# Where the remaining fill units and the first token block's preparation stand, how the first pair begins, and where the rms weight is multiplied

## The chip, the cores and the metric

The kernel runs on one core of a Trainium2 chip. Its engines each work through their own instructions in a fixed order: PE (TensorE) multiplies matrices, PEld is PE's weight load, DVE (VectorE), ACT (ScalarE) and POOL (GpSimd) work on tiles, and SP (SyncE) and ACT issue DMAs, in line with whatever else stands on that engine. An instruction starts when the one before it on its engine lets it and what it waits for on other engines or DMAs is done. The metric is the time of one execution in microseconds (us); lower is better.

## The reference

Linear attention over 8 batches, 8 heads, 576 tokens of 64 dimensions, with 128 random features; its output, as 4608 tokens of 512 channels, goes through an rms norm and a gated layer with 1536 hidden channels. w_gate, w_val, w_out and rms_g follow below as `w_*` and `rms_g`; q, k, v and w_phi are 32-bit floats, the gated layer's weights come as 64-bit floats.

```python
def phi(x):
    proj = np.einsum('bhsd,df->bhsf', x, w_phi)
    proj = proj - np.max(np.abs(proj), axis=-1, keepdims=True)
    return np.concatenate([np.exp(proj), np.exp(-proj)], axis=-1)
q_p, k_p = (phi(q), phi(k))
kv = np.einsum('bhsf,bhsd->bhfd', k_p, v)
z = np.sum(k_p, axis=2)
num = np.einsum('bhsf,bhfd->bhsd', q_p, kv)
den = np.einsum('bhsf,bhf->bhs', q_p, z)[..., None] + 1e-06
x = (num / den)                       # as (B*S, H*D)
rms = np.sqrt(np.mean(x * x, axis=-1, keepdims=True) + 1e-06)
xn = x / rms * rms_g
g = xn @ w_gate
silu = g * (1.0 / (1.0 + np.exp(-g)))
val = xn @ w_val
return (silu * val @ w_out).astype(np.float32)
```

## The kernel before, in words

All products that matter are made from a high and a low part: an operand is cast (`_split`, line 60, on ACT mostly) and the low part is what the cast left over (line 61, DVE or POOL), and a product takes three matmuls.

**Attention** goes over 32 pairs of heads (four per batch) in a pipeline of four steps. In turn i of the main loop `front(i)` transposes k, q and the rests (`rb`, the last 64 tokens of k and q) on PE (L298), projects them (L311 to L313) and takes the largest size off (L315, L318, DVE; tiles `yk`, `yq`, `yr`); `mid(i-1)` makes the exponentials (ACT L338, L342, L375, L376; the low parts `ql` on POOL L380) and sums k's features times v into `acc` (L346, L351), which it splits into `kv0` and `kv1` (h and l); `back(i-2)` makes the numerators and denominators (PE L415, ACT L417) and sends the denominators out and back through memory so that they lie on 64 partitions (`dd`, `dr`, `di`, `rc`: SP L419, L423, L426, L428, with the reciprocal L425 on DVE between); `last(i-3)` divides (`fin`, DVE L442, L443) and stores the result to `xs` (SP). `_merge` puts the pieces of the four steps into one order by their places in the turn.

**Decoding.** The 64-bit weights are turned into 32-bit ones by whole-tile operations (`_decode`, L48 to L55: ACT, DVE, POOL), one piece per turn. The first eight pieces are the first 384 columns of w_gate and w_val; each is then multiplied by the rms weight `g` on DVE (L235) and split into `wf1`.

**Fill.** The products of these 384 columns don't need the rms of x, so they run during attention: `fill` splits a block of 288 tokens of `xs` (16 blocks; `xo`), and each of its six units is 12 matmuls (L474) into a PSUM tile `fp` (two buffers, which `num` and `prep` use too), a copy on ACT (L477, `fo`, three buffers) and a DMA to `gvs` (L478, on SP). `load_x` loads the next blocks on ACT's queue (L142), into one of two x buffers by the block's parity. `quota` hands out units so that some 30 are left when attention ends; the `while` loop does those.

**Preparation.** `prep(bk, x, ...)` (L145 to L165) makes the rms of a block of 384 tokens: four squares on ACT (L147, L150) added on POOL (L151), a sum over the channels on PE (L156, L157), the root on ACT (L159, with a table load), the reciprocal and the scaling on DVE (L160, L162), a cast on ACT and the low part on POOL (tile `xb`). The first block's, `prep(0)`, stands in turn 29 (`PR - 3`), its load in turn 27; `load_x` pauses in between.

**After attention** come the gated layer's other nine column groups for 12 blocks (`gv`, PE L588, with weights loaded through `wc`, ACT queue L564) and the output product (L742). None of that code changes.

A scheduler puts the program's pieces into each engine's order as it expects them to be ready; `late()` ties what stands in it behind the last instructions written so far on ACT, DVE and POOL.

## Time and profile before

| | us |
|---|---|
| time, median of 3 executions | 1333.65 (1332.86 to 1335.17) |
| the profiled execution | 1339.35 |
| its span, first to last instruction | 1337.6 |
| PE busy in it | 1288.5 (96%) |
| PE's mean granted clock | 0.992 |

The profile is of one execution of its own. Rows of the timeline give start, duration, engine, line, operation, tile written and tiles read, and in brackets how long the engine was idle ahead of it and what ended that. Rows of stretches give start and end, length, then the busy time of PE, PEld, DVE, ACT and POOL with counts, PE's granted clock as a share of full speed, the share of the DMA engines and GB/s. A wait row gives who waited for whom, the total, the times and the longest. Line numbers are those of the kernel before.

### The profile page before, as it was taken

What the parts mean: (1) busy time and instruction counts of PE and PEld (TensorE: products, weight loads), DVE (VectorE), ACT (ScalarE), POOL (GpSimd) and SP (SyncE); (2) the same over time, 40 slices, a digit from 0 to 9 for tenths busy, and PEclk for the clock granted to TensorE, in tenths of its full rate; (3) what the DMA queues carried; (4) which work ended last, traced back from release to release, by engine and by line L of the source; (5) the groups of instructions that cost most, each with busy time, mean ns of one, the idle gap of its engine ahead of it and who ended that gap; (6) DMA issues with size and microseconds to landing.
All of it is one profiled execution on the core that took longest, in us unless ns stands there. A gap on an engine that the chain in (4) does not pass through costs nothing.

```text
span 1337.6 us, 25479 instructions
## 1 busy us (share of the span) xinstructions
PE 1288.5 (96%) x9396; PEld 1275.6 (95%) x9396; DVE 885.0 (66%) x1301; ACT 711.0 (53%) x1510; POOL 605.5 (45%) x568
## 2 busy tenths in 40 slices
PE   7989999999999896899999999999999999999998
PEld 7989899999999896899999999999999999999998
DVE  7899788778778773313456656655534498777784
ACT  5988877778778782434344344443333334434332
POOL 3766565555555570000233223233221078788684
PEclk9999999999999898999999999999999999999999
DMA  5555556566555434843454454554433534554451
GB/s 159 127 147 156 161 158 165 167 170 169 157 164 161 123 95 127 249 153 126 141 170 140 157 168 133 166 168 140 133 115 108 183 111 126 150 166 127 142 168 54
DMA packets 204524, 197.22 MB, mean 147 GB/s; under 512 B 69552, under 2 KB 186416, under 8 KB 204400
## 3 DMA queue, kind: packets, MB, share of 16 engines
q1 hardware_dynamic: 186448, 181.44, 45.2%
q10 hardware_dynamic: 17952, 14.16, 3.8%
q8 instruction: 74, 1.21, 0.4%
q14 instruction: 50, 0.41, 0.1%
HBM read 126.04 MB, written 69.50 MB: 146 GB/s over the span
## 4 chain that ended last, share of the span: by engine, by line
PE 57%; DMA 3%; DVE 1%; ACT 0%; issue 0%; POOL 0%; ACTq 0%; SPq 0%; DVEq 0%
PE fp L588 17%; PE gp L588 16%; PE gd L742 6%; PE gz L742 6%; PE gy L742 5%; PE fp L474 4%; PE fp L742 3%; DMA wc<-wvs 1%; DMA gvs<-fo 1%; DMA rc<-di 0%; PE sm L415 0%; DMA dd<-nd 0%; ACT fo L477 0%; POOL s2l L61 0%; DVE a12l L61 0%
## 5 line engine op out<-in xcount | busy, mean ns | idle before, releaser
L380 POOL TENSOR_TENSOR ql<-eq,qh 128x256 fp32r<-128x256 f32 x256 | 217.7, 882 | 67.3 <-issue 39.5
L588 PE MATMUL gp<-xb,wv 128*128 128x384 f32 x864 | 161.9, 334 | 0.8 <-ACT wv L60 0.8
L588 PE MATMUL fp<-xb,wg 128*128 128x384 f32 x864 | 161.0, 334 | 0.0
L573 DVE TENSOR_TENSOR h<-sl,gp 128x384 f32<-128x384 f32 x108 | 59.6, 552 | 144.2 <-PE gp L588 75.6
L588 PEld LDWEIGHTS gp<-xb,wv 128*128 128x128 f32 x864 | 150.7, 188 | 1.0 <-ACT wv L60 1.0
L571 ACT ACTIVATE sl<-fp 128x384 f32<-128x384 f32 x108 | 52.8, 489 | 185.6 <-PE fp L588 170.7
L588 PEld LDWEIGHTS fp<-xb,wg 128*128 128x128 f32 x864 | 150.7, 188 | 0.0
L54 POOL TENSOR_TENSOR wa<-raw,wa 128x192 f32<-128x192 f32 (+1 forms) x112 | 66.2, 613 | 162.2 <-issue 58.6
L351 PE MATMUL acc<-vm,ek 128*128 128x65 f32 x1024 | 131.8, 271 | 0.0
L315 DVE TENSOR_REDUCE mx<-pp 128x4 f32<-128x512 f32 (+1 forms) x160 | 100.6, 632 | 43.0 <-PE pp L313 41.5
L351 PEld LDWEIGHTS acc<-vm,ek 128*128 128x128 f32 x1024 | 128.1, 195 | 0.4 <-ACT ek L338 0.4
L151 POOL TENSOR_TENSOR ss<-ss,sq 128x384 f32<-128x384 f32 x36 | 37.6, 1044 | 160.6 <-ACT sq L150 160.6
L61 POOL TENSOR_TENSOR xb<-x,xb 128x1536 fp32r<-128x1536 f32 x12 | 42.5, 3540 | 132.3 <-ACT xb L60 124.6
L474 PE MATMUL fp<-xo,fg 128*128 128x288 f32 x576 | 92.8, 302 | 5.7 <-ACT fo L477 3.4
L376 ACT ACTIVATE qh<-sm 128x512 fp32r<-128x512 f32 (+1 forms) x192 | 97.3, 507 | 0.0
L474 PE MATMUL fp<-xo,fv 128*128 128x288 f32 x576 | 92.2, 300 | 4.4 <-ACT fo L477 4.4
L311 PE MATMUL pp<-wh,th 128*128 128x256 f32 x288 | 89.0, 310 | 2.7 <-DVE yr L318 2.1
L474 PEld LDWEIGHTS fp<-xo,fg 128*128 128x128 f32 x576 | 81.7, 190 | 7.4 <-ACT fo L477 4.4
L474 PEld LDWEIGHTS fp<-xo,fv 128*128 128x128 f32 x576 | 81.7, 190 | 5.1 <-ACT fo L477 5.1
L61 POOL TENSOR_TENSOR s2l<-st,s2h 128x768 fp32r<-128x768 f32 x18 | 43.5, 2419 | 95.0 <-ACT s2h L60 47.6
L375 ACT ACTIVATE eq<-sm 128x512 f32<-128x512 f32 x128 | 78.4, 612 | 14.1 <-PE sm L364 13.2
L313 PE MATMUL pp<-wh,tl 128*128 128x256 f32 x288 | 83.0, 298 | 1.8 <-DVE tl L61 1.8
(198 smaller groups left out, 3801.8 us busy)
## 6 DMA issues: line engine op xcount, KB each, us to landing
hs<-h SPq DMA_DIRECT2D x144, 192.0 KB
ht<-hs SPq DMA_DIRECT2D x18, 1536.0 KB
gvs<-fo SPq DMA_DIRECT2D x96, 144.0 KB
gvr<-gvs SPq DMA_DIRECT2D x36, 384.0 KB
rc<-di SPq DMA_DIRECT2D x32, 288.0 KB
x<-xs ACTq DMA_DIRECT2D x16, 576.0 KB
x<-xs SPq DMA_DIRECT2D x12, 768.0 KB
kt<-in_k_dram SPq DMA_DIRECT2D x32, 256.0 KB
```

The costliest lines, as they stand in the source:

```text
L54: nc.gpsimd.tensor_tensor(a[:, h], lf[:, h], a[:, h], ALU.mult)
L61: (lo_eng or nc.vector).tensor_tensor(lo, x, hi.bitcast(F32), ALU.subtract)
L311: nc.tensor.matmul(o, th[:, cs], wh, start=True, stop=False)
L313: nc.tensor.matmul(o, tl[:, cs], wh, start=False, stop=True)
L315: nc.vector.tensor_reduce(mx[:, 0:2 * m], pp[:, 0:2 * m], axis=AX.X, op=ALU.max, apply_absolute_value=True)
L351: nc.tensor.matmul(acc[:, sg, h], e[h][:, sg, j], vm[:, h, j], start=False, stop=(h == 1 and j == T0 - 1))
L375: nc.scalar.activation(ei[:, sg], yi, AF.Exp, scale=1.0 - 2.0 * sg)
L376: nc.scalar.activation(hi[:, sg], yi, AF.Exp, scale=1.0 - 2.0 * sg)
L380: nc.gpsimd.tensor_tensor(lo[:, sg, cs], ei[:, sg, cs], hi[:, sg, cs].bitcast(F32), ALU.subtract)
L474: nc.tensor.matmul(fp[:, 0:TF], w, xx[x][:, c], start=(i == 0), stop=(i == 3 * NC - 1))
L588: nc.tensor.matmul(gp[:, 0:T], w, e[:, c], start=(i == 0), stop=(i == 3 * NC - 1))
L742: nc.tensor.matmul(place[n], a[:, kp], w[:, o], start=(first and kp == 0 and i == 0), stop=(kp == KP - 1 and i == 2), skip_group_check=True)
```

## The change

1. In the last three turns of the loop, which have no new pair, nine calls of `more()` are merged among the pieces; each takes one fill unit. Those units' stores and those of the `while` loop go out on ACT's queue; the earlier ones stay on SP's.
2. The first block's preparation stands in the list of fill blocks (`None`), appended in turn 33 (`PR + 1`): it comes after the block then last in the list, and its load with it, on ACT's queue. `load_x` no longer pauses.
3. The first pair transposes and projects k before q and the rests last. The memory of `vr` is set after that of `vm`.
4. The rms weight is multiplied within the decoding: the low half's factor 2^-52 becomes g·2^-52 (`g52`, one new DVE instruction), and the last addition becomes one instruction that multiplies by g and adds. The eight multiplications of L235 go.
5. `late()` no longer ties to a DMA issue.

```diff
@@ -38,21 +38,28 @@
     return raw
 
 
-def _decode(nc, pool, raw, n):
+def _decode(nc, pool, raw, n, scale=None):
+
+
     if raw.dtype == F32:
+        if scale:
+            nc.vector.tensor_scalar(raw, raw, scale[0], None, ALU.mult)
         return raw
     low, high = raw[:, :, 0], raw[:, :, 1]
     p = pool.tile([128, n], I32, name="wp", bufs=2)
     a = pool.tile([128, n], F32, name="wa", bufs=2)
     u, lf = a.bitcast(I32), low.bitcast(F32)
     nc.scalar.mul(a, high.bitcast(F32), REBASE)
-    nc.scalar.mul(lf, low.bitcast(U32), 2.0 ** -52)
+    nc.scalar.mul(lf, low.bitcast(U32), scale[1] if scale else 2.0 ** -52)
     nc.vector.tensor_scalar(p, u, 3, None, ALU.logical_shift_left)
     nc.vector.scalar_tensor_tensor(p, u, -0x80000000, p, ALU.bitwise_and, ALU.bitwise_or)
     nc.vector.tensor_scalar(u, p, -0x00800000, None, ALU.bitwise_and)
     for h in (slice(0, n // 2), slice(n // 2, n)):
         nc.gpsimd.tensor_tensor(a[:, h], lf[:, h], a[:, h], ALU.mult)
-    nc.vector.tensor_tensor(a, p.bitcast(F32), a, ALU.add)
+    if scale:
+        nc.vector.scalar_tensor_tensor(a, p.bitcast(F32), scale[0], a, ALU.mult, ALU.add)
+    else:
+        nc.vector.tensor_tensor(a, p.bitcast(F32), a, ALU.add)
     return a
 
 
@@ -114,6 +121,9 @@
     eps = gl.tile([128, 1], F32, name="eps")
     nc.vector.memset(eps, 1e-6)
     g = gl.tile([128, NC], F32, name="g")
+    g52 = gl.tile([128, NC], F32, name="g52")
+    pad = gl.tile([128, 8], F32, name="pad")
+    nc.vector.memset(pad, 0.0)
 
 
 
@@ -178,7 +188,7 @@
         with ExitStack() as es:
             for eng in LATE:
                 for i in reversed(ins[-300:]):
-                    if i.engine == eng and i.name not in waiting:
+                    if i.engine == eng and i.name not in waiting and not isinstance(i, mybir.InstDMACopy):
                         es.enter_context(tc.issue_after(i))
                         break
             yield
@@ -213,8 +223,9 @@
 
     vms = [const.tile([128, 2, T0, D + 1], F32, name=f"vm{i}") for i in range(3)]
     vrs = [const.tile([128, 2, D + 1], F32, name=f"vr{i}") for i in range(3)]
-    for vm, vr in zip(vms, vrs):
+    for vm in vms:
         nc.gpsimd.memset(vm, 1.0)
+    for vr in vrs:
         nc.gpsimd.memset(vr, 1.0)
         nc.gpsimd.memset(vr[64:128, 0], 0.0)
         nc.gpsimd.memset(vr[0:64, 1], 0.0)
@@ -232,9 +243,8 @@
         for wi, src in enumerate((w_gate, w_val)):
             for c in range(NC):
                 def fill_w(w, wi=wi, c=c):
-                    nc.vector.tensor_scalar(w, w, g[:, c:c + 1], None, ALU.mult)
                     _split(nc, wf1[wi][0][:, c], wf1[wi][1][:, c], w)
-                jobs.append((src[c * 128:(c + 1) * 128, 0:n], n, fill_w))
+                jobs.append((src[c * 128:(c + 1) * 128, 0:n], n, fill_w, (g[:, c:c + 1], g52[:, c:c + 1])))
 
         def keep(jobs, src, dst, r0, c0, n):
             at = slice(r0, r0 + 128), slice(c0, c0 + n)
@@ -259,7 +269,7 @@
             if i + 1 < len(jobs):
                 raws[i + 1] = _fetch(nc, dec, *jobs[i + 1][:2])
             with late():
-                jobs[i][2](_decode(nc, dec, raw, jobs[i][1]))
+                jobs[i][2](_decode(nc, dec, raw, jobs[i][1], *jobs[i][3:]))
         return [lambda i=i: piece(i) for i in range(len(jobs))]
 
     st = {}
@@ -319,6 +329,9 @@
                                     mx[:, 0:2 * m].unsqueeze(2).broadcast_to([128, 2 * m, F]), ALU.subtract)
             d["y"][n, u0 // 2] = y
 
+        if pr == 0:
+            return [lambda: trans("k"), lambda: proj("k", 0), lambda: trans("q"), lambda: proj("k", 2),
+                    lambda: trans("r"), lambda: proj("r", 0), lambda: proj("q", 0), lambda: proj("q", 2)]
         return [lambda: trans("r" if pr else "k"), lambda: trans("k" if pr else "r"),
                 lambda: proj("r", 0), lambda: proj("k", 0), lambda: trans("q"), lambda: proj("k", 2), lambda: proj("q", 0), lambda: proj("q", 2)]
 
@@ -464,7 +477,7 @@
             for c in range(0, NC, 2):
                 _split(nc, *(a[:, c:c + 2] for a in (xx["h"], xx["l"], x)))
 
-        def unit(j, wi):
+        def unit(j, wi, queue):
             js = slice(j * 128, (j + 1) * 128)
             fp = ps_f.tile([128, T], F32, name="fp")
             i = 0
@@ -475,27 +488,40 @@
                     i += 1
             o = xm.tile([128, T], F32, name="fo", bufs=3)[:, 0:TF]
             nc.scalar.copy(o, fp[:, 0:TF])
-            nc.sync.dma_start(out=gvv[j][:, wi, bk * TF:(bk + 1) * TF], in_=o)
-        return [lambda j=j, wi=wi: unit(j, wi) for j in range(J1) for wi in range(2)]
+            queue.dma_start(out=gvv[j][:, wi, bk * TF:(bk + 1) * TF], in_=o)
+        return [lambda q=None, j=j, wi=wi: unit(j, wi, q or nc.sync) for j in range(J1) for wi in range(2)]
 
     PR = B * NP
     early, decs_late = decode_jobs()
     decs = decode_pieces(early, dec)
     RES = 5 * J1 * 2
+    END = 9
+    nxt = []
     units, here = [], []
     dq = quota = 0.0
 
     def load_x():
         while fills and len(here) < 2:
             bk = fills.pop(0)
-            here.append((bk, fetch(bk, TF, nc.scalar)))
+            here.append((bk, fetch(0, T, nc.scalar) if bk is None else fetch(bk, TF, nc.scalar)))
 
     def landed():
-        if here:
+        if here and here[0][0] is None:
+            with late():
+                nxt.append(prep(0, here.pop(0)[1], ps_f, "fp"))
+        elif here:
             units.extend(fill(*here.pop(0)))
+
+    def more():
+        if len(units) <= 3:
+            landed()
+            load_x()
+        if units:
+            units.pop(0)(nc.scalar)
 
     load(0)
     nc.sync.dma_start(out=g, in_=rms_g.rearrange("(c p) -> p c", p=128))
+    nc.vector.tensor_scalar(g52, g, 2.0 ** -52, None, ALU.mult)
     load(1)
     for i in range(PR + 3):
         streams = []
@@ -511,30 +537,29 @@
         dl, decs = decs[:int(dq)], decs[int(dq):]
         dq -= int(dq)
         streams.append(dl)
+        if i >= PR:
+            streams.append([more] * END)
         _merge(streams)
 
-        if i == PR - 3:
-            with late():
-                nxt = prep(0, x0, ps_f, "fp")
-        if len(units) <= 3:
-            landed()
-        if len(units) + (len(fills) + len(here)) * J1 * 2 > RES:
-            quota += (N // TF * J1 * 2 - RES) / (PR - 4)
-            nf = int(quota)
-            quota -= nf
-            now, units[:] = units[:nf], units[nf:]
-            _merge([now])
-        if i == PR - 5:
-            x0 = fetch(0)
-        if not PR - 5 <= i < PR - 3:
-            load_x()
+        if i < PR:
+            if len(units) <= 3:
+                landed()
+            if len(units) + (len(fills) + len(here)) * J1 * 2 > RES:
+                quota += (N // TF * J1 * 2 - RES) / (PR - 4)
+                nf = int(quota)
+                quota -= nf
+                now, units[:] = units[:nf], units[nf:]
+                _merge([now])
+        if i == PR + 1:
+            fills.append(None)
+        load_x()
         if i + 2 < PR:
             load(i + 2)
     while units or here or fills:
         if len(units) <= 6:
             landed()
         now, units[:] = units[:6], units[6:]
-        _merge([now])
+        _merge([[lambda u=u: u(nc.scalar) for u in now]])
         load_x()
     a_ctx.close()
 
@@ -627,7 +652,7 @@
     PRE = 4
     wos_ops = []
     load_gv(0)
-    xb = {0: nxt}
+    xb = {0: nxt[0]}
 
     LAST = [*range(JL, JN), *range(JL)]
     for bk in range(NB):```

The order on PE at the very start, before and then with the change (`kt`, `qt`, `rb` are the loaded k, q and rests; L311 to L313 are L321 to L323 now):

```order
L298 MATMUL sm<-ident,kt 128x128 x4
L298 MATMUL sm<-ident,rb 128x128
L298 MATMUL sm<-ident,qt 128x128 x4
L311 MATMUL pp<-wh,th 128x256
L312 MATMUL pp<-wl,th 128x256
```

```order
L308 MATMUL sm<-ident,kt 128x128 x4
L308 MATMUL sm<-ident,qt 128x128 x4
L321 MATMUL pp<-wh,th 128x256 x2
L322 MATMUL pp<-wl,th 128x256 x2
L308 MATMUL sm<-ident,rb 128x128
L323 MATMUL pp<-wh,tl 128x256
```

The transpose of the rests has moved behind the transposes of k and q and the first four matmuls of k's projection.

The order on DVE around the last pair's `kv1l` (L61, L68 now). L442/L443 (L455/L456) are a `fin`, L425 (L438) the reciprocal of a `back`:

```order
L442 TENSOR_TENSOR nd<-nd,rc 64x576
L443 TENSOR_TENSOR nd<-nd,rc 64x576
L425 RECIPROCAL dr<-dr 128x9
L61 TENSOR_TENSOR kv1l<-acc,kv1h 128x4x65
L61 TENSOR_TENSOR xo<-x,xo 128x576 x2
```

```order
L438 RECIPROCAL dr<-dr 128x9
L62 TENSOR_TENSOR wa<-wp,wa 128x384
L68 TENSOR_TENSOR kv1l<-acc,kv1h 128x4x65
L68 TENSOR_TENSOR xo<-x,xo 128x576 x2
L455 TENSOR_TENSOR nd<-nd,rc 64x576
L456 TENSOR_TENSOR nd<-nd,rc 64x576
L68 TENSOR_TENSOR xo<-x,xo 128x576 x2
L438 RECIPROCAL dr<-dr 128x9
```

`kv1l` now stands ahead of the `fin` and the reciprocal that stood before it.

The order on ACT where the first preparation stands now, in the stage of the remaining units (`fp_8425` is the first unit of block 13, `x_8338` the 384 tokens of the preparation, `x_8441` block 14, `x_8902` the next preparation's tokens); the same instructions stood among the exponentials of turn 29 before:

```order
L490 COPY fo_8438<-fp_8425 128x288
L157 ACTIVATE ss_8443<-x_8338 128x384
L160 ACTIVATE sq_8445<-x_8338 128x384
L491 DMA gvs_58<-fo_8438 128x288
L160 ACTIVATE sq_8448<-x_8338 128x384
L160 ACTIVATE sq_8451<-x_8338 128x384
L67 CAST sq_8455<-ss_8443 128x384
L490 COPY fo_8484<-fp_8471 128x288
L169 ACT_TABLE_LOAD
L169 ACTIVATE ri_8461<-fp_8454,eps_66 128x384
```

```order
L67 CAST xb_8468<-x_8338 128x1536
L490 COPY fo_8532<-fp_8519 128x288
L490 COPY fo_8548<-fp_8535 128x288
L491 DMA gvs_58<-fo_8532 128x288
L491 DMA gvs_58<-fo_8548 128x288
L152 DMA x_8441<-xs_57 128x4x288
L67 CAST xo_8553<-x_8441 128x576 x2
L157 ACTIVATE ss_9026<-x_8902 128x384
L160 ACTIVATE sq_9028<-x_8902 128x384
L490 COPY fo_8571<-fp_8558 128x288
```

The preparation's squares, root and cast have moved from turn 29 in between the copies of the fill units of block 13, and the next preparation's squares stand ahead of the copies of block 14.

## The prediction

> **What bounds the kernel now.** I read the page's busy times first, then PE's waits, then PE, ACT and DVE in the order of time around the longest waits, and last the busy times by stretch.
>
> ```profile
> PE 1288.5 (96%) x9396; PEld 1275.6 (95%) x9396; DVE 885.0 (66%) x1301; ACT 711.0 (53%) x1510; POOL 605.5 (45%) x568
> ```
>
> The span is 1337.6 us, so PE is idle for 1337.6 − 1288.5 = 49.1 us. No matmul is removed by the change. All it can win is part of those 49.1 us and of the time in which PE was granted a lower clock; all it can lose is new idle time of PE. So the sum below is one over PE's gaps.
>
> ```profile
> PE fp L474 <- ACT fo L477: 7.7, 7, 2.0
> PE sm L415 <- DVE kv1l L61: 5.9, 1, 5.9
> PE sm L298 <- DMA rb<-in_q_dram: 2.6, 1, 2.6
> PE pp L311 <- DVE yr L318: 2.1, 1, 2.1
> ```
>
> (Waited in total, times, longest.) The waits stand for four places: the start, a stall near 448, one near 502, and the stage of the remaining fill units from 512 to 620. The same places by stretch (length, then PE, PEld, DVE, ACT and POOL busy, PE's granted clock, DMA share, GB/s):
>
> ```profile
> 0.00:8.00 8.00, 1.67 (x7) 1.33 (x8) 3.61 (x12) 2.48 (x5) 3.96 (x18) 1.00 0.43 118
> 17.00:100.00 83.00, 76.51 (x630) 73.66 (x630) 76.94 (x142) 71.90 (x179) 54.99 (x71) 1.00 0.55 145
> 447.00:451.00 4.00, 1.70 (x11) 1.49 (x10) 3.80 (x6) 2.93 (x9) 1.25 (x2) 0.86 0.35 71
> 451.00:461.00 10.00, 10.00 (x50) 10.00 (x50) 3.61 (x8) 4.65 (x12) 5.38 (x8) 0.54 0.39 118
> 500.00:508.00 8.00, 2.12 (x16) 1.88 (x15) 2.23 (x5) 1.49 (x4) 2.23 (x4) 0.78 0.38 121
> 508.00:512.00 4.00, 4.00 (x19) 4.00 (x20) 1.10 (x2) 0.99 (x2) 0.00 (x0) 0.58 0.14 43
> 512.00:568.00 56.00, 46.55 (x314) 44.61 (x313) 18.01 (x26) 21.11 (x45) 0.00 (x0) 0.97 0.74 215
> 592.00:620.00 28.00, 26.62 (x195) 25.92 (x194) 4.89 (x7) 12.49 (x29) 3.04 (x3) 1.00 0.41 131
> ```
>
> **What goes away: 33.3 us.** *The start.* PE's first projection and its wait for the rests, and the last operand of w_phi on DVE:
>
> ```profile
> 8.37 0.56 PE L311 MATMUL pp<-wh,th 128*128 128x256 f32 x1
> 12.77 0.55 PE L311 MATMUL pp<-wh,th 128*128 128x256 f32 x1 [2.14 <-DVE yr L318]
> ```
> ```profile
> 6.05 0.41 DVE L61 TENSOR_TENSOR wl<-wa,wh 128x256 fp32r<-128x256 f32 x1
> ```
>
> Before, the first projection stands behind the rests' transpose, which waits 2.6 us for its DMA. With k first it can start when wl is there, at 6.05 + 0.41 = 6.46: 8.37 − 6.46 = 1.9 us earlier. The rest's transpose still comes after six of those matmuls, when rb has landed. The 2.14 us wait for yr goes too, since in the new order q's projections lie between. Together 4.0 us. Bounds: 0 (DVE, which sets the pace next, takes it back) to 4.0 plus the remaining 1.0.
>
> *The decoding.* From 17 to 100 DVE is busy 76.94 of 83 us and PE idle for 6.5, so DVE sets part of the pace there.
>
> ```profile
> L235 DVE TENSOR_SCALAR wa<-wa,g 128x384 f32<-128x384 f32 x7 | 4.2, 594 | 0.0
> ```
>
> These multiplications (this row holds the seven in the first 112 us) go; the scaling moves into an ACT and a DVE instruction that exist anyway. The new DVE instruction that scales g (L524) waits for g's DMA, with the yk behind it; g is asked for nearly as early as before, and DVE reaches the place only after its first reductions, so I price that wait at nothing. Of the 4.2 us I take half, 2.0, as PE idles in less than a tenth of the stretch. Bounds 0 and 4.2.
>
> *The stall near 448.* ACT waits for the block of x that the first preparation (prep) squares, its next instructions are what PE waits for, and after that gap PE runs on at half clock:
>
> ```profile
> 448.07 0.52 ACT L147 ACTIVATE ss<-x 128x384 f32<-128x384 f32 x1 [2.38 <-DMA x<-xs]
> ```
> ```profile
> 449.73 1.00 PE L298 MATMUL sm<-ident,kt 128*128 128x128 f32 x4 [2.30 <-ACT qh L376]
> 507.82 0.61 PE L415 MATMUL sm<-qh,kv1l 128*128 128x288 f32 x1 [5.88 <-DVE kv1l L61]
> ```
>
> 2.30 idle, 0.14 × 1.70 = 0.2 at clock 0.86, and 0.46 × 10 = 4.6 at 0.54: 7.1 us. The preparation leaves this place. Lower bound 2.3, if the slow clock has another cause.
>
> *The stall near 502.* The last kv1l stands on DVE behind the dividing of two earlier pairs, and these wait for DMAs:
>
> ```profile
> 502.53 0.75 DVE L442 TENSOR_TENSOR nd<-nd,rc 64x576 f32<-64x576 f32 x1 [6.49 <-DMA rc<-di]
> 507.27 0.22 DVE L425 RECIPROCAL dr<-dr 128x9 f32<-128x9 f32 x1 [3.21 <-DMA dr<-dd]
> ```
>
> In the new order kv1l stands ahead of both (shown above with the change), so the 5.88 us go, with 0.22 × 2.12 = 0.5 and 0.42 × 4 = 1.7 of slow clock: 8.0.
>
> *512 to 620.* Idle 56 − 46.55 = 9.45 and 28 − 26.62 = 1.4, and 0.03 × 46.55 = 1.4 of clock: 12.2. I take all of it off, and price what the new stage has in its place. Sum: 4.0 + 2.0 + 7.1 + 8.0 + 12.2 = 33.3.
>
> **What comes: 28.8 us.** Fill units now fill the last pairs' gaps, but the first preparation moves to the end, where fewer instructions cover it. A unit takes 1.60 us of PE (two starts below). The prices:
>
> ```profile
> 599.57 1.76 PE L474 MATMUL fp<-xo,fg 128*128 128x288 f32 x12
> 601.17 1.76 PE L474 MATMUL fp<-xo,fv 128*128 128x288 f32 x12
> ```
> ```profile
> 596.60 0.52 ACT L147 ACTIVATE ss<-x 128x384 f32<-128x384 f32 x1 [2.43 <-DMA x<-xs]
> 599.77 0.40 ACT L477 COPY fo<-fp 128x288 f32<-128x288 f32 x1 [0.53 <-PE fp L474]
> 602.24 0.52 ACT L60 CAST sq<-ss 128x384 fp32r<-128x384 f32 x1
> 608.11 1.25 ACT L60 CAST xo<-x 128x576 fp32r<-128x576 f32 x2
> ```
> ```profile
> 478.21 1.28 ACT L159 ACT_TABLE_LOAD   x1
> 479.51 0.58 ACT L159 ACTIVATE ri<-fp,eps 128x384 f32<-128x384 f32 x1
> 487.50 1.56 ACT L60 CAST xb<-x 128x1536 fp32r<-128x1536 f32 x1
> ```
> ```profile
> 480.12 2.55 DVE L160 RECIPROCAL ri<-ri 128x384 f32<-128x384 f32 x1 [1.05 <-ACT ri L159]
> 484.00 2.68 DVE L162 SCALAR_TENSOR_TENSOR x<-x,g,ri 128x384 f32<-128x384 f32 x4
> ```
> ```profile
> 492.14 3.49 POOL L61 TENSOR_TENSOR xb<-x,xb 128x1536 fp32r<-128x1536 f32 x1
> ```
>
> *A, 6.6.* On PE the preparation's sum of squares stands right behind the first unit of block 13. On ACT its chain starts only behind that unit's copy: 0.40, then 602.24 + 0.52 − 596.60 = 6.2 from ss to the cast. Nothing else is queued ahead on PE. The bounds are near, 6.2 and 6.6.
>
> *B, 5.6.* After the next unit: copy 0.40, table 1.28, ri 0.58, reciprocal 2.55, scaling 2.68, cast 1.56 = 9.05 us, against four units = 6.4 on PE: 2.65. Then three matmuls (0.5) and POOL's 3.49 for the low part: 3.0 more. Lower bound 4, if ACT overlaps the starts.
>
> *C, 4.2.* From the end of POOL's low part: the x of block 14 can be loaded only now (same buffer). A load takes from its issue on the queue below to 596.60, 5.2 us for 768 KB; three quarters of that would be 3.9 for these 576 KB, and I put 4.4.
>
> ```profile
> 591.43 0.37 SPq L142 DMA_DIRECT2D x<-xs  x1
> 507.68 1.42 DVE L61 TENSOR_TENSOR xo<-x,xo 128x576 fp32r<-128x576 f32 x2
> ```
>
> Then cast 0.68 and low parts 1.42, then the next preparation's load 5.2 on the same buffer, and its ss, sq and the fill copy behind them 1.4: 13.1. PE has until then the first gp group of 33 matmuls (5.7) and two units (3.2): 8.9. Bounds 3 and 5.
>
> *D, 1.7.* The last block's cast (1.25) stands behind a copy (0.40) that PE's unit has just freed. Bounds 0 and 1.7.
>
> *The stage from the last pair's end to block 13, 8.5.* The fill copies leave SP's queue for ACT's, and no longer wait there behind rc and xs; but the weight tiles' casts stand on the same ACT.
>
> ```profile
>   DMA wc<-wgs: 7.5, 5
>   DMA wc<-wvs: 1.6, 4
> ```
> ```profile
> 531.77 0.75 DVE L442 TENSOR_TENSOR nd<-nd,rc 64x576 f32<-64x576 f32 x1 [6.98 <-DMA rc<-di]
> ```
>
> ACT waited 9.1 us for these landings before; gp groups covered it, now there are none. Two PSUM buffers let PE run ahead of the copies, so I take half: 4.6. The x of block 11 is loaded on ACT behind a split that DVE has only after such a wait for rc: 6.5 (the row at 502.53) less two and a half units in hand, 4.0 = 2.5. With clock as before, 1.4: 8.5. Bounds 2 and 11.
>
> *Slow clock, 2.2.* After 507.82 it cost 1.7 + 0.5. Three gaps here are as long as the one at 449.73 or longer, but what is slow behind A and B runs into waits whose end POOL and DMAs set; only the spell behind C is paid. Bounds 0 and 4.6. Sum: 8.5 + 6.6 + 5.6 + 4.2 + 1.7 + 2.2 = 28.8.
>
> The trace shows ek ending at about 478.2 and the table load at 478.21 with ri right behind it, so a table costs 1.3. [...]
>
> **The sum.** 33.3 − 28.8 = 4.5 us less. The profiled execution took 1339.35 (1.75 more than its span, 5.70 more than the median 1333.65): 1339.35 − 4.5 = 1334.85, and against the median 1329.15. I say 1329.2. About 0.2% (2.7 us) is what a measurement tells from no change.
>
> **Rivals.** *Slower: ACT becomes the queue of everything.* 53 fill transfers now sit among ACT's copies, casts and, in the last three pairs, exponentials; an issue there can wait for an older transfer such as rc, and all behind it wait: the copies that free PE's PSUM, and x's loads. rc lands 6.5 to 7.0 us late in the rows at 502.53 and 531.77; less two units (3.2) that is 3.3 to 3.8 for each of three pairs, 10.6 in all: 1329.2 + 10.6 = 1339.8. It wins over the forecast's gain from 4.5 on, that is with two of the three pairs. For it speaks that ACT's order is fixed; against, that these queues had half their time free (21.11 busy of 56).
>
> *Clearly faster: the new units cover more.* If the weight loads land early and DVE is off the path at the start, the stage costs 2 in place of 8.5 and the decoding gives 4.2: 1329.2 − 6.5 − 2.2 = 1320.5. Against it speaks that A, B and C are serial.
>
> *No change: the slow clock was not the stall's.* PE ran at 0.54 for ten us after only 2.30 idle, but at 0.58 for four after 5.88. If the long spell has another cause it turns up elsewhere: 1329.2 + 4.6 = 1333.8. [...]
>
> **Chances.** Forecast (1325 to 1334) 0.43, ACT's queue 0.26, covered 0.16, clock 0.15. Faster: all of covered, 0.33 of the forecast, 0.03 of the clock case: 0.52. Same: 0.10 of the forecast and 0.12 of the clock case: 0.22. Slower: ACT's queue, 0.26. The forecast's own range is 1325 to 1334; that of 8 in 10 reaches half into both outer cases: 1320 to 1339.
>
> **What would show it.** Right: the 5.88 wait of L415's counterpart is gone and full clock near 448; PE's first projection near 6.5; in the tail a PE gap of about 6.6 before the sum of squares, one of 2.7 and one of 3.0 before the first gp matmuls, one of about 4 after the first gp group. Wrong: PE waits for copies in the last three pairs, with DMA issues on ACT waiting for rc; gaps A to C missing or twice as long; PE idle between 17 and 100 as much as before.

## The result: slower by 1.5%

The changed kernel took 1355.31 us (median of 4 executions, 1354.0 to 1356.95) against 1333.68 before on the same chip: a ratio of 1.0149, 95% interval 1.0124 to 1.0174. I had said 1329.2, with 1339 as the upper end. Its profiled execution took 1354.0 with a span of 1352.2, 14.6 us more than the span before (that one was a long execution of the kernel before, so the medians lie further apart than the spans).

I compare the two traces by PE's *lost* time: the length of a stretch less PE's busy time times its granted clock. The rows of the changed kernel have the columns of the rows of stretches above:

```profile
0.00:80.00 80.00, 71.18 (x542) 68.20 (x542) 66.04 (x128) 62.47 (x151) 45.40 (x71) 1.00 0.53 143
80.00:200.00 120.00, 107.73 (x829) 104.77 (x830) 96.33 (x169) 91.84 (x228) 71.31 (x87) 0.93 0.56 149
420.00:480.00 60.00, 60.00 (x498) 60.00 (x498) 45.37 (x77) 45.78 (x115) 30.26 (x40) 1.00 0.52 152
480.00:640.00 160.00, 138.12 (x944) 132.21 (x943) 55.66 (x82) 72.72 (x160) 31.17 (x33) 0.96 0.49 149
1120.00:1300.00 180.00, 180.00 (x1519) 180.00 (x1518) 1.00 0.49 150
```

Of the kernel before (the last row of each counts the matmuls of the output phase alone):

```profile
0.00:80.00 80.00, 68.83 (x541) 66.42 (x542) 65.59 (x128) 61.38 (x151) 43.47 (x70) 1.00 0.55 142
80.00:200.00 120.00, 112.36 (x909) 107.65 (x908) 105.12 (x190) 97.94 (x242) 77.55 (x96) 1.00 0.58 156
420.00:480.00 60.00, 56.20 (x426) 55.21 (x425) 46.52 (x80) 46.33 (x113) 37.70 (x46) 0.91 0.44 122
480.00:640.00 160.00, 143.29 (x996) 140.42 (x995) 55.47 (x76) 71.27 (x153) 20.48 (x21) 0.97 0.51 156
1120.00:1300.00 180.00, 180.00 (x1560) 180.00 (x1559) 1.00 0.47 145
```

| stretch | lost before | lost now | difference | predicted |
|---|---|---|---|---|
| 0 to 80 | 11.2 | 8.8 | −2.4 | −4.0 and part of −2.0 |
| 80 to 200 | 7.6 | 19.8 | **+12.2** | the rest of −2.0 |
| 420 to 480 | 8.9 | 0.0 | −8.9 | −7.1 |
| 480 to 640 | 21.0 | 27.4 | +6.4 | 28.8 − 20.2 = +8.6 |
| output phase | | | **+6.4** | 0 |

Two rows were in no step of the prediction. Between 80 and 200 us PE waits (120 − 107.73 = 12.3 us idle), and its clock falls to half (0.50 from 88 to 92 and from 120 to 124). In the 180 us of the output phase that are shown PE is busy without a gap in both kernels and does 1519 matmuls where it did 1560: from the start of its first to the start of its last matmul the phase takes 272.3 us in place of 265.9, at full clock (1.00 in both), with not one instruction changed. The other rows came within some 2 us of what was predicted. From 200 to 420 us 2.0 were lost before and 0.8 now, and some 2 of the 14.6 us stand in no row. The tail by its parts:

```profile
PE fp L487 <- ACT fo L490: 8.6, 9, 2.0
PE fp L166 <- ACT sq L67: 6.6, 1, 6.6
PE gp L613 <- POOL xb L68: 2.7, 1, 2.7
PE gp L613 <- ACT xb L67: 1.3, 1, 1.3
```
```profile
579.84 0.69 PE L166 MATMUL fp<-sq,ones 128*128 128x384 f32 x1 [6.65 <-ACT sq L67]
592.12 0.79 PE L613 MATMUL gp<-xb,wv 128*128 128x384 f32 x3 [1.27 <-ACT xb L67]
595.64 8.62 PE L613 MATMUL gp<-xb,wv 128*128 128x384 f32 x33 [2.72 <-POOL xb L68]
609.07 1.86 PE L487 MATMUL fp<-xo,fg 128*128 128x288 f32 x12 [1.63 <-ACT fo L490]
```

(PE's waits from 496 on, and PE in order of time.) Gap A is 6.65 us, B 1.27 + 2.72, C 1.63. C is shorter than its 4.2 because PE was slow ahead of it (clock 0.50 from 596 to 600 and 0.82 from 600 to 604): the 33 matmuls took 8.62 us, not 5.7, so the slow clock ran into a wait that other engines end. B is shorter than its 5.6 for several small reasons: DVE's scaling took 2.21 us in place of 2.68, and PE had 7.6 us of work in place of 6.4 until then (583.21 to 590.85), because one matmul of the preparation (L167) stood ahead of the four units and the clock was 0.93 in that time.

The new loss, on DVE of the changed kernel near 115 us, and in PE's stretches there:

```profile
113.72 1.07 DVE L60 SCALAR_TENSOR_TENSOR wa<-wp,g,wa 128x384 f32<-128x384 f32 x1 [0.17 <-POOL wa L58]
114.72 0.68 DVE L328 TENSOR_TENSOR yq<-pp,mx 128x512 f32<-128x512 f32 x1
115.32 0.74 DVE L455 TENSOR_TENSOR nd<-nd,rc 64x576 f32<-64x576 f32 x1
116.08 1.17 DVE L456 TENSOR_TENSOR nd<-nd,rc 64x576 f32<-64x576 f32 x1
117.29 0.21 DVE L438 RECIPROCAL dr<-dr 128x9 f32<-128x9 f32 x1
117.42 0.37 DVE L68 TENSOR_TENSOR kv0l<-acc,kv0h 128x260 fp32r<-128x260 f32 x1
```
```profile
112.00:116.00 4.00, 1.93 (x10) 1.28 (x10) 3.79 (x6) 4.00 (x10) 4.00 (x6) 1.00 0.97 215
116.00:120.00 4.00, 2.16 (x9) 2.16 (x10) 3.94 (x8) 3.70 (x8) 2.68 (x3) 0.59 0.57 129
120.00:124.00 4.00, 4.00 (x21) 4.00 (x20) 1.59 (x3) 0.50 (x1) 1.98 (x3) 0.50 0.37 127
```

```profile
113.10 0.63 PE L377 MATMUL sm<-ident,yq 128*128 128x128 f32 x4 [1.60 <-DVE yq L328]
117.84 0.61 PE L428 MATMUL fp<-qh,kv0l 128*128 128x288 f32 x1 [1.96 <-DVE kv0l L68]
```

PE waits for `yq` behind the new long L60 and for `kv0l` behind a `fin` and a reciprocal. It is busy 1.93 and 2.16 us of two stretches of four; its clock is 0.59 in the second of them and 0.50 in the next. It is the picture of the stall near 502 that the prediction read in the kernel before, at a new place.

### The profile page after: what moved, and what is told of

It reads as the page before. It is cut to its first block, busy times and chain, and to the rows that moved or that the text cites. A ratio compares the mean times of both kernels' runs of the same rounds, so it can differ in the third digit from the quotient of the medians.

```text
span 1352.2 us, 25401 instructions
## 1 busy us (share of the span) xinstructions
PE 1301.2 (96%) x9396; PEld 1287.3 (95%) x9396; DVE 883.9 (65%) x1295; ACT 715.6 (53%) x1509; POOL 607.5 (45%) x568
## 4 chain that ended last, share of the span: by engine, by line
PE 78%; DVE 6%; DMA 5%; ACT 3%; POOL 1%; issue 1%; ACTq 0%; SPq 0%; DVEq 0%; POOLq 0%
PE fp L613 17%; PE gp L613 16%; PE fp L487 7%; PE gd L767 5%; PE gz L767 5%; PE acc L364 5%; PE gy L767 5%; PE sm L428 4%; PE fp L767 3%; DMA gvs<-fo 2%; PE fp L428 2%; PE sm L377 2%; PE pp L323 2%; PE pp L321 2%; PE pp L322 1%; PE sm L308 1%
## 5 line engine op out<-in xcount | busy, mean ns | idle before, releaser
L393 POOL TENSOR_TENSOR ql<-eq,qh 128x256 fp32r<-128x256 f32 x256 | 223.7, 906 | 83.8 <-issue 45.7
L613 PE MATMUL gp<-xb,wv 128*128 128x384 f32 x864 | 164.2, 338 | 4.0 <-POOL xb L68 2.7
L613 PE MATMUL fp<-xb,wg 128*128 128x384 f32 x864 | 161.4, 334 | 0.0
L613 PEld LDWEIGHTS gp<-xb,wv 128*128 128x128 f32 x864 | 153.3, 191 | 4.5 <-POOL xb L68 3.0
L613 PEld LDWEIGHTS fp<-xb,wg 128*128 128x128 f32 x864 | 150.6, 188 | 0.4 <-ACT fo L490 0.3
L58 POOL TENSOR_TENSOR wa<-raw,wa 128x192 f32<-128x192 f32 (+1 forms) x112 | 62.9, 583 | 143.7 <-ACT sl L596 54.9
L68 POOL TENSOR_TENSOR xb<-x,xb 128x1536 fp32r<-128x1536 f32 x12 | 42.4, 3535 | 143.7 <-ACT xb L67 136.1
L487 PE MATMUL fp<-xo,fv 128*128 128x288 f32 x576 | 95.4, 303 | 6.1 <-ACT fo L490 6.0
L487 PE MATMUL fp<-xo,fg 128*128 128x288 f32 x576 | 92.7, 301 | 3.9 <-ACT fo L490 2.6
L321 PE MATMUL pp<-wh,th 128*128 128x256 f32 x288 | 88.9, 311 | 2.8 <-ACT th L67 1.7
L487 PEld LDWEIGHTS fp<-xo,fv 128*128 128x128 f32 x576 | 82.3, 191 | 7.6 <-ACT fo L490 7.5
L487 PEld LDWEIGHTS fp<-xo,fg 128*128 128x128 f32 x576 | 80.6, 188 | 6.5 <-ACT fo L490 4.5
L323 PE MATMUL pp<-wh,tl 128*128 128x256 f32 x288 | 84.5, 304 | 0.0
L322 PE MATMUL pp<-wl,th 128*128 128x256 f32 x288 | 81.5, 285 | 0.0
```

Source lines behind the costliest of these rows:

```text
L321: nc.tensor.matmul(o, th[:, cs], wh, start=True, stop=False)
L322: nc.tensor.matmul(o, th[:, cs], wl, start=False, stop=False)
L323: nc.tensor.matmul(o, tl[:, cs], wh, start=False, stop=True)
L393: nc.gpsimd.tensor_tensor(lo[:, sg, cs], ei[:, sg, cs], hi[:, sg, cs].bitcast(F32), ALU.subtract)
L487: nc.tensor.matmul(fp[:, 0:TF], w, xx[x][:, c], start=(i == 0), stop=(i == 3 * NC - 1))
L613: nc.tensor.matmul(gp[:, 0:T], w, e[:, c], start=(i == 0), stop=(i == 3 * NC - 1))
```

## The experiments

All ratios are to the kernel before, timed on the same chip, with 95% intervals. "Output" is the time from the first to the last matmul of the output phase in that run's profile, "80 to 200" PE's lost time there, summed over stretches of 20 us.

**Is it the scaled decoding?** The multiplication goes back behind the decoding:

```diff
-                jobs.append((src[...], n, fill_w, (g[:, c:c + 1], g52[:, c:c + 1])))
+                    nc.vector.tensor_scalar(w, w, g[:, c:c + 1], None, ALU.mult)
+                jobs.append((src[...], n, fill_w))
```

> The changed kernel, but the rms weight is multiplied on DVE after the decoding, as before (the scaled weights g52 are still computed, so every tile keeps its place). Theory S (the scaled decoding's longer DVE instruction stands ahead of kv0l and makes PE wait until its clock drops): the two half-clock spells near 88 and 120 us go, about 10 us, so 1345. Theory F (the new order of the first pair shifted the phases of everything behind it, and that makes the waits): the spells stay, 1355 within 3.

1.0132 (1.0095 to 1.0169); 80 to 200: 21.9; output 272.3. The decoding isn't needed for the loss. The other way round, the kernel before with the scaled decoding alone:

> The kernel before with the scaled decoding alone (and the tiles g52 and pad, so that all tiles stand as in the changed kernel). Theory S: half-clock spells in the first 140 us, 8 to 12 us more; with theory A another 6 in the output phase: 1348 to 1352. Theory F: the decoding alone gives 0 to 4 us, and 1330 to 1334 without A, 1336 to 1340 with A.

1.0117 (1.0073 to 1.0161); 80 to 200: 27.8; output 272.4. It is enough for the loss. Theory S had nearly this time, but not the loss that stays without the decoding; theory F had that one, but not this; there must be something that both this and the first pair's order bring about. That order alone:

```diff
+        if pr == 0:
+            return [lambda: trans("k"), lambda: proj("k", 0), lambda: trans("q"), ...]
-    for vm, vr in zip(vms, vrs):
+    for vm in vms:
         nc.gpsimd.memset(vm, 1.0)
+    for vr in vrs:
```

> The kernel before with the first pair's new order alone (k, q, rests last; the memory of vr set after vm). By my sum 4.0 us less (0 to 5). Theory F (the order shifts the phases behind it): start 3 us shorter, but 8 to 12 us more lost between 80 and 200: 1339 to 1343.

1.0045 (1.0029 to 1.0062); 80 to 200: 17.8; output 265.9. It too is enough, and slower by itself, where the prediction had 4.0 us less.

**Is it the addresses?** `g52` and `pad` take a slot each of the memory's first pool, and nearly every tile behind them moves by 64 bytes.

```diff
-    pad = gl.tile([128, 8], F32, name="pad")
+    pad = gl.tile([128, 24], F32, name="pad")
```

> The changed kernel with 64 bytes more of padding, so that all tiles behind it stand 128 bytes, not 64, from where they stood before. Theory A (the output phase is slower because its operands moved by 64 bytes within 128): the output phase takes 266 us again as in the kernel before, 6 us less in all, 1349. Theory C (its rate is a matter of the execution, not of addresses): it stays at 272 or changes without pattern.

1.0152 (1.0111 to 1.0192); output 272.7. Then the kernel before once more, the kernel before with an unused tile (`pad = gl.tile([128, 16], ...)`, 64 bytes; and `[128, 64]`, 256 bytes), and the changed kernel with `g52` in the free half of g's slot:

```diff
-    g = gl.tile([128, NC], F32, name="g")
-    g52 = gl.tile([128, NC], F32, name="g52")
-    pad = gl.tile([128, 8], F32, name="pad")
-    nc.vector.memset(pad, 0.0)
+    gg = gl.tile([128, 2 * NC], F32, name="g")
+    g, g52 = gg[:, 0:NC], gg[:, NC:2 * NC]
```

> The kernel before once more, unchanged, for a second profile of it beside the others. Theory A (addresses): output phase 266 us and some 8 us of PE lost between 80 and 200, as in its first profile. Theory C (the execution or the chip): output phase 272 us as in all five kernels run since; if the 12 us more between 80 and 200 are also the chip's, 20 us lost there too, and the difference between the two kernels is then to be looked for at the end alone.

0.9999 (0.9978 to 1.0021); output 265.9, 80 to 200: 11.0. So neither loss is the chip's or the execution's; between 80 and 200 two profiles of this one kernel lost 7.6 and 11.0, so that figure is known to some 3 us.

> The kernel before with one more tile of 64 bytes, unused, so that every tile behind it stands where it stands in the changed kernel; nothing else. Theory A: output phase 272 us and 20 us lost between 80 and 200, 1345 to 1352. Theory C: the time of the kernel before within 3 us on the same chip.

1.0032 (1.0009 to 1.0055); output 272.3, 80 to 200: 9.5. Theory A holds for the output phase alone.

> The kernel before with an unused tile of 256 bytes in place of the 64. If the output phase depends on addresses within 256 bytes, it takes 266 us again; if any shift against the tiles that are placed from the other end of the memory costs it, 272.

1338.99 in its one execution; output 265.9. The matmuls of the output phase in 180 us with 64 bytes, then with 256:

```profile
1120.00:1300.00 180.00, 180.00 (x1518) 180.00 (x1518) 1.00 0.47 145
```
```profile
1120.00:1300.00 180.00, 180.00 (x1560) 180.00 (x1559) 1.00 0.47 144
```

> The changed kernel with g52 in the unused half of g's slot and no padding, so that all tiles but yk and yr stand where they stood before. Theory A: output phase 266 us and the loss between 80 and 200 down from 20 to 8 us: 18 us less, 1337. Theory C: 1355 within 4.

1.0078 (1.0050 to 1.0107); output 265.9, 80 to 200: 20.4. The output phase's 6.4 us are shown to be a matter of where its tiles lie: 64 or 128 bytes of shift cost them, 0 and 256 don't (256 in a single execution). Which operands it is was not tried. The 12 us are something else.

**What is the tail worth by itself?** First the changed kernel with the preparation moved back to turn 29:

```diff
+        if i == PR - 3:
+            with late():
+                nxt.append(prep(0, x0, ps_f, "fp"))
...
-        if i == PR + 1:
-            fills.append(None)
-        load_x()
+        if i == PR - 5:
+            x0 = fetch(0)
+        if not PR - 5 <= i < PR - 3:
+            load_x()
```

> The changed kernel, but the first preparation stands in turn 29 with its load in turn 27, as before. By my sum of the tail: the gaps A, B, C and part of the slow clock go (6.6 + 5.6 + 4.2 + 2.2 = 18.6) and the stall near 448 comes back (2.3 to 7.1): 12 to 16 us less, 1340. If the rival holds that the tail costs the same wherever the preparation stands, 1353 to 1357.

1.0061 (1.0037 to 1.0086), median 1343.9: 0.0088 or 11.8 us less than the changed kernel, at the lower end of what I expected. Then without the decoding, `g52`, `pad` and the first pair's order, so that only the tail's parts are left; with the preparation late, with it in turn 29, and this with all stores on SP (`units.pop(0)()` in `more`, `_merge([now])` in the `while` loop):

> The changed kernel without the scaled decoding, without g52 and the padding, and with the first pair's old order: what is left is the nine fill units per turn, ACT's queue for their stores, the first preparation at the end and the late() rule. All tiles stand where they did in the kernel before, and DVE's first 200 rows are its order word for word. Theory N (near-equal orders of the crowded first 200 us, and the addresses, made the loss): output phase 266 us, 8 to 11 us lost between 80 and 200 and no half-clock spells there; the stall near 448 gone (3 to 7), the tail 25 to 28 in place of 19 to 20: the time of the kernel before within 4 us. If the fills' own change disturbs the first part, 1345 or more.

1.0009 (0.9988 to 1.0029); 80 to 200: 7.7; nothing lost from 420 to 480. The time came as expected, though the tail lost 32.6 us (below) and not 25 to 28.

> As the run with all but the tail undone, and the first preparation back in turn 29: only the nine fill units per turn, ACT's queue and the late() rule remain. From the run with the preparation moved back (12 us lost from 480 on, in place of 19 to 20 before): 6 to 8 us less than the kernel before, if theory N holds. If ACT's queue was the rival's trouble, no gain.

0.9954 (0.9937 to 0.9971), median 1332.02.

> The same as that one, with the stores of all fill units on SP's queue, as in the kernel before. If the gain of the end comes from units that fill PE's gaps, it stays within 2 us; if it comes from the stores no longer standing behind rc and xs on SP, 4 to 8 us of it go.

0.9950 (0.9932 to 0.9968), median 1330.01. The stretch from 480 to 640, late preparation first, then in turn 29:

```profile
480.00:640.00 160.00, 136.94 (x905) 131.88 (x904) 50.80 (x75) 71.38 (x155) 27.42 (x28) 0.93 0.49 146
```
```profile
480.00:640.00 160.00, 148.28 (x1028) 145.54 (x1027) 59.25 (x80) 74.40 (x156) 23.90 (x22) 0.98 0.51 157
```

Lost 32.6 against 14.7 us; some 8 of these 18 come back near 448. Nine fill units in each of the last three turns, with the `late()` rule, which was not tried by itself, gain half a per cent; the late preparation costs 0.55% and takes all of that; and whose queue carries the stores makes no difference that can be measured (0.9954 and 0.9950). In these three the first 200 us lose what they lost before: the tail's parts don't disturb them.

**What do the decoding and the first pair's order have in common?** The order of DVE, in short: K is a low part of kv (`kv0l`, `kv1l`), F the two multiplications of a `fin`, r the reciprocal of `inv`, for the first nine pairs or so:

```
before           KKrKFrKFrKFrFrKKFrKFrKFr
changed          KKrFrKKFrFrKKFrFrKKFrKFr
first pair only  KKrKFrKFrFrKKFrFrKKFrKFr
decoding only    KKrKFrKFrFrKKFrFrKKFrKFr
tail only        KKrKFrKFrKFrFrKKFrKFrKFr
decoding undone  KKrKFrKFrKFrFrFrKKFrKFrK
```

(The last is the changed kernel without the scaled decoding.) The common turn is K F r. Where F r comes ahead of K (`FrK` in place of `KFr`) the numerators of the next pair wait for a `fin`. Before, it happens once (near 95 us, where 3.8 us are lost between 80 and 100) and at the last pair (the stall near 502); in the slower kernels two or three times in the first seven pairs, or, with the decoding undone, once with three F r ahead of K (near 113 us; 8.3 us are lost between 100 and 120 there). So I wrote `fin` and `inv` behind the split in each turn:

```diff
-                (0.5, lambda: num(1, 1)), (0.79, inv)]
+                (0.5, lambda: num(1, 1)), (1.07, inv)]
-        return [(0.65, fin)]
+        return [(1.06, fin)]
```

in the changed kernel with the old addresses, in the kernel before, and in two of the mixtures; DVE's order is then K F r up to the last pair in all of them.

> The changed kernel with the old addresses, and with the dividing (fin) and the reciprocal (inv) written behind the split of k and v in each turn, so that on DVE every kv0l and kv1l stands ahead of them; in the changed kernel three of the first seven stand behind two of these. Theory K (a low part of kv that stands behind a fin and a reciprocal makes PE wait, and two such waits drop PE's clock): the half-clock spells near 88 and 120 us go and the loss between 80 and 200 falls from 20 to 8 us or less: 12 us below 1349, 1337. Theory P (any crowded order there loses as much): 1347 to 1351.

1.0156 (1.0109 to 1.0202); 80 to 200: 14.0, but 200 to 420: 10.2, where 0.7 was lost.

> The kernel before with that writing order alone. Theory K: its own swapped place near 95 us goes (3.8 us of idle time between 80 and 100 down to 1), and the stall of 5.9 us near 502 with its slow clock (8.0): 8 to 11 us less, 1327. Theory P: within 3 us of the kernel before.

1.0088 (1.0056 to 1.0120). The stall near 502 did go (12.6 us lost from 480 to 640), but 9.8 are lost from 200 to 420, in place of 2.0, and 15.8 from 80 to 200, in place of 7.6 and 11.0. PE's longest waits there are:

```profile
PE pp L311 <- DVE yr L318: 7.1, 2, 3.9
```

> Only the nine fill units per turn and the late() rule, with stores on SP's queue, the first preparation in turn 29, and that writing order. Theory K: 3 us less than the same without the writing order (the place near 95; the stall near 502 is gone there already): 0.993 of the kernel before.

1.0051 (1.0027 to 1.0075); 80 to 200: 15.7, where the same without that writing order lost 8.2.

> The whole change with the old addresses, that writing order, and the first preparation in turn 29. If the prediction's other terms hold (start 3 us, decoding 0 to 4, the end 6 to 8), 0.988 to 0.993 of the kernel before, and the lowest of all.

1.0021 (0.9999 to 1.0043). All four missed. PE's waits of the first of them from 200 to 480 show why:

```profile
PE pp L319 <- DVE yr L326: 7.2, 4, 2.9
PE fp L485 <- DVE xo L68: 4.1, 2, 2.7
```

The `fin` written last stands ahead of the next pair's `yr` now, and PE waits for that, as it does between 80 and 200 in the row above. The place had been put right, and a new wait put behind it: putting every low part of kv first is not by itself the cure. So it was done for the first pairs alone (1.06 for pairs below 4, 1.07 below 5, the old places else); DVE's order is K F r again, by itself, in the pairs after.

> The changed kernel with the old addresses, and with fin and the reciprocal written behind the split of k and v for the first four pairs alone (five for the reciprocal); on DVE every low part of kv then stands ahead of them, and from the sixth pair on the writing order is the changed kernel's. When this was done for all pairs, fin made the rests wait instead, and 10 us went between 200 and 420. Theory K: loss between 80 and 200 from 20 to 8 to 12 us, and between 200 and 420 no more than 2: 1338 to 1341, against 1349. Theory P: 1347 to 1352.

1.0001 (0.9985 to 1.0017), median 1337.15; 80 to 200: 8.3, 200 to 420: 1.4. PE's stretches, with the old addresses alone and with the first pairs' place put right as well:

```profile
80.00:100.00 20.00, 17.63 (x115) 16.89 (x116) 13.68 (x26) 14.49 (x36) 11.75 (x14) 0.83 0.38 101
100.00:120.00 20.00, 14.92 (x114) 14.06 (x113) 17.69 (x30) 15.67 (x37) 11.52 (x15) 0.91 0.72 174
120.00:140.00 20.00, 19.72 (x144) 19.56 (x144) 14.79 (x28) 12.32 (x32) 11.48 (x14) 0.84 0.43 127
```
```profile
80.00:100.00 20.00, 18.55 (x154) 18.15 (x155) 18.93 (x34) 16.61 (x41) 15.15 (x18) 1.00 0.56 138
100.00:120.00 20.00, 17.28 (x132) 16.89 (x131) 16.36 (x28) 14.88 (x39) 10.02 (x13) 0.91 0.74 186
120.00:140.00 20.00, 19.25 (x164) 19.04 (x163) 18.48 (x31) 17.67 (x45) 12.19 (x16) 1.00 0.55 148
```

PE's longest waits between 80 and 140, in the same two kernels:

```profile
PE fp L426 <- DVE kv0l L68: 3.6, 2, 2.0
PE sm L375 <- DVE yq L326: 2.7, 2, 2.3
```
```profile
PE fp L426 <- ACT kv0h L67: 2.4, 1, 2.4
PE sm L375 <- ACT ek L349: 1.0, 1, 1.0
```

The waits for `yq` and `kv0l` are gone, and with them the spells of half clock near 88 and 120 (0.50 from 88 to 92 and from 120 to 124 with the old addresses alone, now 1.00); one wait for `kv0h` with a short slow spell is left near 110 (0.74 from 108 to 112, 0.84 from 112 to 116). At last this with the preparation in turn 29:

> The same with the first preparation in turn 29. If the three causes (addresses, order of the first pairs, the preparation at the end) add up, 20.4 - 10 us less between 80 and 200 and 9 us less for the preparation than with the old addresses alone: 1328 to 1332, 0.990 to 0.996 of the kernel before.

0.9930 (0.9898 to 0.9962), median 1327.58 (1319.97 to 1333.52), and 12.4 us lost from 480 to 640 (160 − 149.07 × 0.99):

```profile
480.00:640.00 160.00, 149.07 (x1025) 146.06 (x1024) 55.58 (x77) 70.67 (x149) 25.40 (x23) 0.99 0.55 167
```

It is faster than both kernels and has the lowest median of all, though its interval overlaps that of the tail's fill units alone (0.9950). From the changed kernel to this one in steps: 1.0149, less 0.0071 with the old addresses, less 0.0077 with the place put right, less 0.0071 with the preparation in turn 29. Taken singly elsewhere the addresses measured 0.0032 and the preparation 0.0055 and 0.0088, so the steps are known to about that.

## Why the prediction was wrong

- **The step that failed: the decoding ("Of the 4.2 us I take half, 2.0 ... Bounds 0 and 4.2"), and the start beside it ("Bounds: 0 ... to 4.0 plus the remaining 1.0").** Both priced the instructions that go, with 0 as the worst case. The two edits made the scheduler set DVE's order anew, and in three of the first seven pairs a low part of kv fell behind a `fin` and a reciprocal. That cost 12.2 us between 80 and 200, shown by putting the place right: 20.4 to 8.3. I had quoted the very same pattern at the last pair, priced its removal at 8.0, and didn't look for it in the other 31 pairs of the order that I had before me. The gain was too large as well: the addition that takes over the scaling (L60) takes 950 ns in the mean, L55 and L235 together took 683 + 594 in the first 112 us, so some 330 ns go with each multiplication and not 594; the longer instruction was priced at nothing. One sign of being wrong that I had named came true: PE idles between 17 and 100 nearly as much as before (6.2 us now, 6.5 then), and at a lower clock, as the row of the changed kernel shows:

```profile
17.00:100.00 83.00, 76.83 (x611) 74.78 (x610) 69.43 (x126) 70.22 (x172) 53.16 (x67) 0.96 0.48 130
```

- **A term that wasn't there: the addresses.** I priced `g52` as one DVE instruction and gave `pad` no price, and set out from "all it can lose is new idle time of PE"; here PE lost 6.4 us without idling. The 64 bytes by which they move the other tiles cost them, in the output phase. This is shown; why 64 and 128 cost and 0 and 256 don't stays open.
- **The start was right in its mechanism and a little large**: PE's first projection came at 5.75 and no longer waits for `yr`; 2.4 us are left at 80, not 4.0, one swapped pair near 55 us (a wait of 1.6 for `kv0l`) having taken part of it back. The rests' transpose comes after four matmuls of the projection, not six. With the first pair's order alone nothing of the gain is left at 80 us: 12.0 us are lost up to there, summed over stretches of 20 us (11.2 before, 8.8 in the changed kernel), 2.3 of them by a clock of 0.83 in the first 20.
- **The tail was right in its order and its sum, in its parts less so**: 27.4 us lost where 28.8 were priced for what comes, and A 6.65 for 6.6. But B and C came 4.2 us shorter than priced (1.27 + 2.72 + 1.63 for 9.8), D 1.1 for 1.7, and the slow clock cost 5.5 (0.04 × 138.12) for 2.2 + 1.4; that the sum is within 1.4 us is in part luck. The conclusion that lay in this, that the late preparation takes the whole gain of the fill units, I drew only as a sum.
- **The stall near 448** went (8.9 us in the profile). It is not worth that in each execution. Of ten profiles with the preparation in turn 29 and the old writing order at that place, seven lose 6.5 to 11.2 us from 420 to 480, summed over stretches of 20 us, at a clock of 0.71 to 0.83 in the slowest of these, and three (the kernel before once more, 3.1, the preparation moved back, 2.9, and the scaled decoding alone, 3.3) lose only the idle time, at a clock of 1.00.
- **The base.** The forecast was 26.1 us too low. 19.1 of these are between the profiles (14.6 more, in place of 4.5 less). The other 7.0 are that the profiled execution of the kernel before was 5.7 longer than its median and that of the changed kernel 1.3 shorter; I had taken the same 5.7 us off the forecast.
- **The rivals.** ACT's queue didn't cost what the rival said: stores on ACT or SP make 0.9954 and 0.9950 with the preparation in turn 29, and in the changed kernel, with 56 of these stores on ACT (not 53), PE's waits for the copies are 8.6 us in nine, none over 2.0. With the late preparation the queue was not changed by itself. "Clearly faster" didn't come true: with three causes taken out the ratio is 0.9930, where 1320.5 would be 0.990. The rival of the slow clock's cause was about a real thing: PE's clock fell near 117 (0.59 from 116 to 120) in the second of two stretches of half idle, though no single wait was over 2.0 us, and not in the kernel before at 92 to 100, where PE was busy 2.76 and 2.56 us of four (rows below). How much idle time brings the lower clock, and whether idle time alone does, no run here shows.

```profile
92.00:96.00 4.00, 2.76 (x24) 2.56 (x23) 3.59 (x8) 4.00 (x11) 2.79 (x5) 1.00 0.58 142
96.00:100.00 4.00, 2.56 (x19) 2.16 (x19) 3.94 (x8) 3.33 (x8) 3.47 (x5) 1.00 0.69 212
```

- **The table load** cost in the tail what was priced, 1.28 us: ri starts 1.30 us after it (583.86 and 585.16), as it did before (478.21 and 479.51).

```profile
583.86 1.28 ACT L169 ACT_TABLE_LOAD   x1
585.16 0.58 ACT L169 ACTIVATE ri<-fp,eps 128x384 f32<-128x384 f32 x1
```

## What to carry to other kernels

Where a scheduler sets the order, a small edit is paid for in the order of everything near it: find the pattern behind each stall of the trace, and look for it in the whole new order, not only at the place that one hopes to mend. A new small tile can move all tiles behind it; compare a phase that the edit doesn't touch, by its matmuls in a fixed stretch, before explaining anything else. And take a combined change apart: here one part (fill units in the last turns) gave half a per cent, and the others hid it.

## What the hardware showed that I had not expected

- In 180 us at full clock (1.00) PE does 1560 matmuls of the output phase or 1519, 2.6% fewer, by 64 bytes of address, and it doesn't idle in either. The phase of the gated layer's column groups (`gv`) kept its pace: the reciprocals of its first preparations stand 37.8 us apart in both kernels (635.4 and 673.2 before, 643.6 and 681.4 now), and from 700 to 1000 us PE does 1717 of its matmuls (L588, L613) in both.
- Half clock after waits of at most 2.0 us: in two stretches of four us PE worked less than 2.2 us each; its clock was 0.59 in the second and 0.50 and 0.63 in the two that followed. From 112 to 128 that is 3.9 us of idle time and 4.4 of clock.
- Executions of one and the same kernel spread over 1331 to 1343 us across these runs, wider than the 1332.9 to 1335.2 first shown; spells of slow clock that come in some executions and not in others are part of that (8.9 and 3.1 us lost from 420 to 480 in the two profiles of the kernel before).
